# Score heads kept in different row strips, twelve exp tiles in flight, and head outputs turned by DMA: one change to a two-layer FFT-filter and attention kernel

## The chip, the core and the metric

The kernel runs on one core of a Trainium2 chip. A core has a matrix engine (TensorE, PE in the profile; its weight loads are listed as PEld), a vector engine (VectorE, DVE), a scalar engine (ScalarE, ACT), a general engine (GpSimd, POOL) and a sync engine (SP), which here only issues DMAs. Each engine runs its own list of instructions strictly in order and waits on semaphores for the others. The metric is the device time of one execution in microseconds (us).

## The reference

The input is a sequence of 2048 rows of 512 numbers in bf16. Two pairs of layers follow one another. The first layer of a pair filters in the frequency domain, the second is attention with 32 heads that share one key and one value head. Each works on the layer-normed rows and is added to them.

```python
S, D, H = 2048, 512, 32; Dh = 16
def _A_ref(x, w_r, w_i):
    X = rfft2(x) * (w_r + 1j * w_i)
    return irfft2(X, s=(S, D))
def _B_ref(x, wq, wk, wv, wo):
    q = (x @ wq).reshape(B, S, H, Dh).transpose(0, 2, 1, 3)
    k = x @ wk                      # one key head, 16 wide
    v = x @ wv
    scores = einsum("bhqd,bkd->bhqk", q, k) * Dh ** -0.5
    p = softmax(scores)
    o = einsum("bhqk,bkd->bhqd", p, v)
    return o.transpose(0, 2, 1, 3).reshape(B, S, H * Dh) @ wo
x = A_x
for _ in range(2):
    x = x + _A_ref(layernorm(x), A_w_r, A_w_i)
    x = x + _B_ref(layernorm(x), B_wq, B_wk, B_wv, B_wo)
```

## The kernel before, in words

The rows stay in SBUF in `x_sb`. The filter is done with matrix products against cosine and sine tables (`mm1`, `mid`, `inv`, `y_mm`) and radix-2 and radix-4 sums on VectorE (`radix2`, `radix4`). Nearly all the time goes into the attention.

**Units of attention work.** The queries are cut into four blocks `qb` of 512. The 32 heads are cut into four groups `g` of 8, and each group into two halves `par`, so a block is `(qb, g, par)`: 512 queries, 4 heads. There are 32 blocks a layer. The 2048 keys are cut into 16 chunks `kc` of 128. A unit is one head of one block against one key chunk: 64 units a block, 2048 a layer, 4096 in all.

**Scores.** `Emit.scores` (L1313 of the profile) multiplies a 32x128 slice of the keys (`KA` or `KB`) with a 32x512 slice of the queries. The head number `h` (0 to 3) picks the strip of 32 rows of the array that the product uses. Products in different strips run beside each other; two in the same strip run one after the other. In this text a slot is a set of such products in different strips, which the array does at one time.

**Exponentials, on two engines.** A pair of units goes to one of two two-bank PSUM tiles `sa` and through one exp on ScalarE (`Emit.exp`, L1318), which writes a 128x1024 bf16 tile `e2`. There are 13 such tiles, and the planner keeps at most `E_BUFS = 8` of them between scores and use. A single unit goes to a one-bank tile `b` and through VectorE: `p1` (L1325) makes a 16-bit integer whose bits are an approximate exponential. For every four units, two more integer tiles with an added constant are made (`phase`), nearly always on GpSimd (L1329); the three together average the error of the approximation out.

**Products with the values.** `Emit.pv` (L1335) multiplies a 128x32 slice of the values (16 columns of values, the rest ones, so that the softmax sum comes along) with the exponentials. Here the head picks a strip of 32 columns of the array. A ScalarE unit needs one such product, a VectorE unit three.

**Closing a block.** When all products of a block are there, VectorE turns the PSUM result in 32x32 squares (`evac`, L1342), and for each pair of blocks takes the reciprocal of the sums (`recip`, L1347), multiplies (`mul`, L1353) and turns the bf16 result back (`norm`, L1362) into `OT`, which is the stationary operand of the output projection `proj` (L1366). When the four groups of a `qb` are there, `close_rows` projects and adds the rows (`close_x`, L1248); in the first pair the front of the next filter layer (`mm1`, L1099, and `bn`, L1028) then follows among the attention work. A pair of row tiles is turned for that through DRAM: `turn_x` (L1070) writes `way`, `turned` (L1063) reads it with a transposing DMA.

**The order.** Nothing is scheduled by the compiler. `Plan` is a planner in Python with a price for every instruction. It keeps one clock for each engine and always emits the step that can start first. `do_scores` fills up to five score requests in a row, and for each takes the engine that would run dry first (`deadline`). `Attn.peek` says which heads of the current key chunk come next: for ScalarE the first two that are left, for VectorE one, preferably in a strip that is still free in the present slot. ScalarE gets no new scores while `live["ACT"]` has reached `bufs["ACT"]`. `round` gathers products with the values: it waits for four different heads unless the block is finished or a buffer limit is reached. `fill` puts products with zeros (L1010, L1014) on TensorE where it would do too little to keep its clock up. The result is one fixed list of instructions per engine.

Of the kernel before, what the change touches and what calls it, by code (L numbers as in the profile page):

```python
# [52 lines left out]
    return tabs  # L53


def radix2(nc, sd, x, piece):

    nc.vector.tensor_tensor(out=sd[:, 2 * piece:2 * piece + 2, :], in0=x[:, 0:2, :], in1=x[:, 2:4, :],
                            op=ALU.subtract if piece else ALU.add)


def radix4(nc, sd, x, half, o, piece):
# [53 lines left out]
class Plan:  # L116
# [12 lines left out]
    PORT = True  # L129
    POOL_LAG = 2600.0  # L130
    E_BUFS = 8
    T_BUFS = 4
    WIN = 3413.0
    WARM = 3500.0
# [11 lines left out]
    PATIENT = 1000.0  # L146
    URGE = 150.0
    TURN = 7000.0
    EARLY_SD = 0
    STARVED = 12000.0  # L150

    def __init__(self):
        self.t = {"PE": 0.0, "ACT": 0.0, "DVE": 0.0, "POOL": 0.0}
        self.mode = ""
        self.sa = [0.0, 0.0]
        self.bank = [0.0] * self.NB
        self.use = [None] * self.NB
        self.bg = {"PE": [], "ACT": [], "DVE": [], "POOL": []}
        self.n = 0
        self.hist = []  # L160
        self.at = None
        self.act_fifo, self.p1_fifo, self.ph_fifo, self.pool = [], [], [], []
        self.pv = []
        self.half = None
        self.live = {"ACT": 0, "DVE": 0}
        self.bufs = {"ACT": self.E_BUFS, "DVE": self.T_BUFS}
        self.dve_last = ""
        self.acc_of = {}
        self.bg_last = self.port = 0.0
        self.ranks, self.base = None, 0  # L170

    def ranked(self, which):
# [24 lines left out]
    def run(self, goal):  # L197
        while not goal():
            best = None
            for c in (self.pe_next(), self.act_next(), self.dve_next(), self.pool_next()):  # L200
                if c is not None and (best is None or c[0] < best[0]):
                    best = c
            best[1](best[0], *best[2:])


# [210 lines left out]
    def round(self):  # L416
        at = self.at
        avail = []
        free = self.slot_free("b")
        for e in sorted(self.pv, key=lambda e: e[:2]):  # L420
            if (e[2] in self.acc_of or free is not None) and e[4] // 4 in at.v_ready:
                avail.append((max(e[0], at.v_ready[e[4] // 4]),) + e[1:])
        if not avail:
            return None
        b0 = min(e[2] for e in avail)
        t0 = 0.0 if b0 in self.acc_of else free
        heads, sel = set(), []
        for e in avail:
            if e[2] == b0 and e[3] not in heads:
                heads.add(e[3])  # L430
                sel.append((max(e[0], t0),) + e[1:])
        if len(sel) < 4 and b0 + 1 in self.acc_of:
            for e in avail:
                if e[2] == b0 + 1 and e[3] not in heads:
                    heads.add(e[3])
                    sel.append(e)
        full = any(self.live[k] >= self.bufs[k] for k in ("ACT", "DVE"))
        return sel if len(sel) == 4 or self.made(b0) or full else None

    def made(self, b, h=None):  # L440
# [147 lines left out]
class Attn:  # L588
# [25 lines left out]
    def peek(self, kind, strips=()):  # L614


        cur = self.cur[kind]
        if not cur and self.groups:
            b, kc = self.groups[0]
            cur = [(b, kc, h) for h in range(4)]  # L620
        if not cur:
            other = self.cur["DVE" if kind == "ACT" else "ACT"]
            cur = other if kind == "DVE" or len(other) > 1 else []
        if kind == "ACT":
            return cur[:2]
        return sorted(cur, key=lambda u: u[2] in strips)[:1]

    def take(self, kind, us):
        if not self.cur[kind] and self.groups:
# [30 lines left out]
    def done(self, b, slot, end):  # L660
        p, em = self.plan, self.em
        qb, g, par = self.blocks[b]
        self.left.discard(b)
        m = Mark("PE", end, slot)
        ev = p.add("DVE", 630.0, [m], lambda k: em.evac(self, b, slot), give=(m,), prio=-3)
        self.evac[b] = self.evac_last = ev
        if par == 0:
            return
        tail = 0.0 if b >= len(self.blocks) - 2 else 5000.0
        rc = p.add("DVE", 260.0, [ev, self.evac[b - 1]], lambda k: em.recip(self, b), lazy=tail)  # L670
        mu = p.add("DVE", 600.0, [rc], lambda k: em.mul(self, b), lazy=tail, port=True)
        no = p.add("DVE", 626.0, [mu], lambda k: em.norm(self, b), lazy=tail)
        self.evac[b] = no
        if g == 3:
            self.layer.close_rows(qb, [self.evac[8 * qb + 2 * i + 1] for i in range(4)])


class Layer:
# [83 lines left out]

    def add_middle(self):
        p, em = self.plan, self.em
        self.mid, self.fil = [], []
        for u in range(4):
            evs, two = [], u in self.two

            if two:
                outs = [((0, 2), (0, 1), 0), ((1, 3), (0, 1), 2)]  # L770
            else:
                outs = [((0, 1, 2, 3), (0, 1), 0), ((0, 1, 2, 3), (2, 3), 2)]
            if u % 2:
# [27 lines left out]
    def add_back(self):  # L801
        p, em, at = self.plan, self.em, self.at
        left = [T]
        for t in range(T):
# [53 lines left out]
            def v_got(k, t=t):  # L858
                at.v_ready[t] = k.end + p.LAT[k.eng]
                left[0] -= 1  # L860
                if left[0] == self.EARLY:
                    at.dve_on = True
                    at.dve_from = k.end - 2000.0
# [61 lines left out]
class Emit:  # L925


    def __init__(self, ctx, tc, ins, out):
# [21 lines left out]
        self.part = const.tile([P, 2], F32, name="part")  # L950
        self.wv = const.tile([P, NC, DH], BF, name="wv")
        self.tc = tc
        self.e2 = [const.tile([P, 1024], BF, name=f"e2_{i}") for i in range(13)]
        self.idle, self.home, self.writer = list(range(13)), {}, {}
        self.WO = const.tile([P, 4, D], BF, name="WO")
        self.junk = const.tile([P, 512], BF, name="junk")
        self.eps = const.tile([P, 1], F32, name="eps")
# [197 lines left out]
    def turn(self, L, u, piece):  # L1155
        if piece == 0:
            L.sd_of[("x", u)] = self.t4([4, 512])
        radix2(self.nc, L.sd_of[("x", u)], L.X[u], piece)
        if piece:
            L.X[u] = L.sd_of.pop(("x", u))  # L1160

# [14 lines left out]

    def radix_d(self, L, u, piece):
        if piece == 0:
            L.Dz[u] = self.t4([4, 512], tag="xd", bufs=4)
        radix2(self.nc, L.Dz[u], L.X[u], piece)  # L1180

    def load_it(self, L, t):
        L.IT[t] = self.t4([4, 640], tag="it", bufs=2)
# [2 lines left out]
    def inv(self, L, t, b, j, slot, ks):  # L1186
# [4 lines left out]
        for k in ks:  # L1191
            u = 2 * j + k
            for a in range(2):
                for i in range(2):
                    w = 128 * (3 - (t * a + i) % 4)
                    z = L.Dz[u][:, 2 * (t % 2) + a, 256 * i + 128 * b:256 * i + 128 * b + 128]
                    self.nc.tensor.matmul(ps[:, k, :], lhsT=z, rhs=L.IT[t][:, u, w:w + 256], start=(a == 0 and i == 0),
                                          stop=(a == 1 and i == 1), skip_group_check=True)

    def inv0(self, L, b, j, slot, k):  # L1200

# [155 lines left out]
    def norm(self, at, b):  # L1357
# [3 lines left out]
            at.OT[qb] = self.t4([4, 512])  # L1361
        self.nc.vector.transpose(out=at.OT[qb][:, g, :], in_=on.rearrange("p a h d -> p (a h d)"))  # L1362

    def proj(self, at, t, r, slot, g0, g1):
        for g in range(g0, min(g1, 4)):
            self.nc.tensor.matmul(self.ps(slot), lhsT=at.OT[t][:, g, r * P:(r + 1) * P], rhs=self.WO[:, g, :],  # L1366
# [90 lines left out]
```

The softmax here doesn't subtract the row's maximum and nothing guards it: scores larger than these inputs give would overflow.

## Time and profile before

| what | value |
|---|---|
| runs shown | 1343.59, 1343.7 and 1344.19 us; median 1343.7 us |
| the profiled execution | span 1341.6 us, first to last instruction; it has no separate device time, so the span stands 2.1 us under the median of the runs |
| granted TensorE clock | 1.000 of full speed |
| attention of the first layer, last value slice (L1291) to last block closing (L1342) | 109.5 to 681.7 us |
| attention of the second layer, likewise | 774.9 to 1333.3 us |
| exp instructions on ScalarE (L1318) | 1232 |
| `p1` instructions on VectorE (L1325) | 1632 |
| transposes `norm` on VectorE (L1362) | 32 |

The page gives busy time by engine. Instructions of one engine overlap a little in its records: an exp lasts 1087 ns on average (group rows of L1318), but the next one can start 904 ns after it. So a wait shorter than about 180 ns does not show as idle time of ScalarE. Where this text speaks of a pitch, it is the time from the start of one instruction to the start of the next on that engine, read from the trace. Times of stretches are counted from the start of the span.

### The profile page before, as it was taken

How to read it: one execution, taken by the hardware profiler on the slowest of the kernel's cores; microseconds unless marked ns; L12 is line 12 of the kernel's file. 1: busy time of each engine (PE TensorE's matmuls, PEld its weight loads, DVE VectorE, ACT ScalarE, POOL GpSimd, SP SyncE). 2: the span in 40 equal slices, each digit the busy share in tenths (PEclk: the TensorE clock that was granted, in tenths of full speed). 3: DMA queues.
4: the chain of work that ended last, by engine and by line, in shares of the span. 5: the costliest groups of instructions: out<-in, count | busy, mean ns of one | idle time of the engine just before them, and what ended most of it. 6: DMA issues, size and time to landing. Idle time of an engine off the chain costs nothing. (4 is left out here: it accounts for less than half of the span.)

```text
span 1341.6 us, 31639 instructions
## 1 busy us (share of the span) xinstructions
PE 1310.9 (98%) x13046; PEld 428.0 (32%) x13046; DVE 1291.2 (96%) x2317; ACT 1225.7 (91%) x1390; POOL 849.7 (63%) x831
## 2 busy tenths in 40 slices
PE   9999999999999999999999999999999999999998
PEld 4642222222222222222246422222222222322222
DVE  6998999999999999999969999999999999999998
ACT  6478999999999999899954889999999999998996
POOL 0004777767776777667720068777777777876775
PEclk9999999999999999999999999999999999999999
DMA  9100000010001000100051000000000000000000
GB/s 292 41 1 1 2 1 2 2 33 1 2 2 33 1 2 2 32 2 2 1 165 41 1 1 1 2 2 6 13 2 2 6 13 2 2 1 17 1 1 17
DMA packets 29041, 25.16 MB, mean 19 GB/s; under 512 B 8672, under 2 KB 27616, under 8 KB 28896
## 3 DMA queue, kind: packets, MB, share of 16 engines
q1 hardware_dynamic: 28608, 22.58, 5.7%
q8 instruction: 102, 1.67, 0.5%
q10 hardware_dynamic: 288, 0.56, 0.1%
q14 instruction: 43, 0.35, 0.1%
HBM read 17.89 MB, written 3.67 MB: 16 GB/s over the span
## 5 line engine op out<-in xcount | busy, mean ns | idle before, releaser
L1313 PEld LDWEIGHTS <-KB 32*128 32x128 bf16 x2048 | 83.9, 91 | 224.0 <-issue 218.5
L1313 PEld LDWEIGHTS <-KA 32*128 32x128 bf16 x2048 | 82.3, 91 | 226.0 <-issue 217.8
L1335 PEld LDWEIGHTS <-vs_108 128*32 128x32 bf16 x2464 | 96.3, 94 | 111.3 <-issue 107.7
L1335 PEld LDWEIGHTS <-vs_109 128*32 128x32 bf16 x1632 | 96.3, 94 | 71.4 <-issue 69.0
L1335 PEld LDWEIGHTS <-vs_111 128*32 128x32 bf16 x1632 | 72.1, 94 | 72.7 <-issue 67.6
L1335 PEld LDWEIGHTS <-vs_110 128*32 128x32 bf16 x1632 | 70.0, 94 | 75.4 <-issue 71.9
L1329 POOL INT64_ADD w_1384<-w_1383 x1 | 1.0, 1041 | 110.5 <-DVE w_1383 L1325 110.5
L1329 POOL INT64_ADD w_10948<-w_10947 x1 | 1.0, 1039 | 97.7 <-DVE w_10947 L1325 97.7
L1318 ACT ACTIVATE e_2_86<-sa_65 128x1024 bf16<-128x1024 f32 x47 | 51.1, 1088 | 4.5 <-PE sa_64 L1313 4.0
L1318 ACT ACTIVATE e_12_96<-sa_65 128x1024 bf16<-128x1024 f32 x47 | 51.1, 1087 | 4.5 <-PE sa_64 L1313 4.1
L1318 ACT ACTIVATE e_5_89<-sa_65 128x1024 bf16<-128x1024 f32 x49 | 53.2, 1086 | 1.8 <-PE sa_64 L1313 1.0
L1318 ACT ACTIVATE e_7_91<-sa_64 128x1024 bf16<-128x1024 f32 x50 | 54.7, 1095 | 0.0
L1318 ACT ACTIVATE e_9_93<-sa_65 128x1024 bf16<-128x1024 f32 x49 | 53.2, 1086 | 1.6 <-PE sa_64 L1313 0.8
L1318 ACT ACTIVATE e_0_84<-sa_65 128x1024 bf16<-128x1024 f32 x47 | 51.7, 1101 | 3.2 <-PE sa_64 L1313 3.1
L1318 ACT ACTIVATE e_6_90<-sa_65 128x1024 bf16<-128x1024 f32 x49 | 53.1, 1083 | 1.5 <-PE sa_64 L1313 1.0
L1318 ACT ACTIVATE e_1_85<-sa_64 128x1024 bf16<-128x1024 f32 x50 | 54.2, 1083 | 0.0
L1318 ACT ACTIVATE e_3_87<-sa_65 128x1024 bf16<-128x1024 f32 x47 | 51.4, 1093 | 2.3 <-PE sa_64 L1313 2.0
L1318 ACT ACTIVATE e_11_95<-sa_65 128x1024 bf16<-128x1024 f32 x47 | 51.4, 1093 | 2.2 <-PE sa_64 L1313 1.9
L1318 ACT ACTIVATE e_4_88<-sa_65 128x1024 bf16<-128x1024 f32 x49 | 53.0, 1081 | 0.1
L1318 ACT ACTIVATE e_12_96<-sa_64 128x1024 bf16<-128x1024 f32 x48 | 52.7, 1099 | 0.2 <-PE sa_64 L1313 0.2
L1318 ACT ACTIVATE e_10_94<-sa_64 128x1024 bf16<-128x1024 f32 x49 | 52.5, 1072 | 0.1
L1318 ACT ACTIVATE e_3_87<-sa_64 128x1024 bf16<-128x1024 f32 x48 | 52.2, 1086 | 0.1
(4003 smaller groups left out, 6246.9 us busy)
## 6 DMA issues: line engine op xcount, KB each, us to landing
it<-const_IT SPq DMA_DIRECT2D x8, 640.0 KB, 6.3
x_sb<-in_A_x_dram SPq DMA_DIRECT2D x4, 512.0 KB, 6.9
out_dram<-x_sb SPq DMA_DIRECT2D x16, 128.0 KB, 1.8
way<-x_sb SPq DMA_DIRECT2D x6, 256.0 KB, 2.2
tab_PH<-const_PH ACTq DMA_DIRECT2D x1, 512.0 KB, 5.1
w_123<-const_FT SPq DMA_DIRECT2D x1, 512.0 KB, 8.8
w_128<-const_FT SPq DMA_DIRECT2D x1, 512.0 KB, 8.5
tab_PS<-const_PS SPq DMA_DIRECT2D x1, 512.0 KB, 7.9
```

Of the source, the lines that this page charges most:

```text
L1313: self.nc.tensor.matmul(o, lhsT=KX[rs, kc * P:(kc + 1) * P], rhs=at.QT[qb][rs, g, :], start=True, stop=True, skip_group_check=True)
L1318: self.wrote("ACT", e, self.nc.scalar.activation(out=e, in_=self.ps(slot), func=ACT.Exp, scale=SCALE))
L1329: self.nc.gpsimd.int64_add(t[p][:, 0:n].bitcast(U64), t[0][:, 0:n].bitcast(U64), DELTA[p] * FOUR)
L1335: self.nc.tensor.matmul(self.ps(slot)[32 * h:32 * h + 32, :], lhsT=V[:, kc, :], rhs=rhs, start=first, stop=last, skip_group_check=True)
```

## The change

Three things are done to the planner and the emitter, with what they need around them.

First, `peek` takes the strips into account for both engines: ScalarE's two heads are chosen among those whose strips are free in the present slot, and, after that, so that they differ from the last heads that the other engine still holds.

Second, the limit on ScalarE tiles in flight becomes 12 from the moment that all value slices of a layer are there, and goes back to 8 where the next filter layer's middle part is planned. The pool grows from 13 to 21 tiles of `e2`. The sums of `radix_d`, which had four tiles `xd` of their own, now use two `e2` tiles each and give each back after its last use.

Third, for all pairs of blocks but the last of a layer the transpose `norm` is replaced by `norm_dma`: four DMAs write the result to DRAM in runs of 64 bytes, and a transposing DMA reads it back into `OT`. The planner reckons with 25 us from `mul` until the projection may use it. All five are issued on SP.

If no engine has anything that it may do, the planner now lets `round` go with fewer than four heads once.

```diff
 class Plan:
     E_BUFS = 8
+    E_LATE = 12
+    OUT_TURN = 25000.0
...
 def run(self, goal):
+            if best is None:
+                assert not self.force
+                self.force = True
+                continue
+            self.force = False
             best[1](best[0], *best[2:])
...
 def round(self):
-        full = any(self.live[k] >= self.bufs[k] for k in ("ACT", "DVE"))
+        full = self.force or any(self.live[k] >= self.bufs[k] for k in ("ACT", "DVE"))
...
 def peek(self, kind, strips=()):
+        taken = lambda x: {u[2] for u in self.cur[x]} if 0 < len(self.cur[x]) <= 2 else ()
         if kind == "ACT":
-            return cur[:2]
-        return sorted(cur, key=lambda u: u[2] in strips)[:1]
+            d = taken("DVE")
+            return sorted(cur, key=lambda u: (u[2] in strips, u[2] in d))[:2]
+        a = taken("ACT")
+        return sorted(cur, key=lambda u: (u[2] in strips, u[2] in a))[:1]
...
 def done(self, b, slot, end):
-        no = p.add("DVE", 626.0, [mu], lambda k: em.norm(self, b), lazy=tail)
+        if b < len(self.blocks) - 2:
+            no = Mark("DMA", None)
+
+            def turned(k):
+                em.norm_dma(self, b)
+                no.end = k.end + p.OUT_TURN
+
+            mu.then = turned
+        else:
+            no = p.add("DVE", 626.0, [mu], lambda k: em.norm(self, b), lazy=tail)
...
 def add_middle(self):
+        p.bufs["ACT"] = p.E_BUFS
...
 def v_got(k, t=t):
+                if left[0] == 0:
+                    p.bufs["ACT"] = p.E_LATE
...
-        self.e2 = [const.tile([P, 1024], BF, name=f"e2_{i}") for i in range(13)]
+        self.e2 = [const.tile([P, 1024], BF, name=f"e2_{i}") for i in range(21)]
...
 def radix_d(self, L, u, piece):
         if piece == 0:
-            L.Dz[u] = self.t4([4, 512], tag="xd", bufs=4)
-        radix2(self.nc, L.Dz[u], L.X[u], piece)
+            L.Dz[u] = [[self.t2([2, 512]), 4] for _ in range(2)]
+            for z, _ in L.Dz[u]:
+                self.writer.pop(self.home[id(z)][0], None)
+        radix2(self.nc, L.Dz[u][piece][0], L.X[u], piece)
...
 def inv(self, L, t, b, j, slot, ks):
+            d = L.Dz[u][t % 2]
+            d[1] -= 1
+            if d[1] == 0:
+                self.free2(d[0])
...
+    def norm_dma(self, at, b):
+        qb, g, par = at.blocks[b]
+        on = at.raw.pop((qb, g))
+        if g == 0:
+            at.OT[qb] = self.t4([4, 512])
+        way = self.way.tile([512, P], BF, name="onw", tag="onw")
+        rows = way.rearrange("(a q) (h c) -> h q a c", q=32, c=32)
+        for h in range(4):
+            self.nc.sync.dma_start(out=rows[h], in_=on[32 * h:32 * h + 32].rearrange("p a h d -> p a (h d)"))
+        self.nc.sync.dma_start_transpose(out=at.OT[qb][:, g:g + 1, :], in_=way)
```

More of the change, by code (lines that the diff above doesn't have):

```diff
@@ L53, in host_tables, with radix2 @@
     return tabs
-def radix2(nc, sd, x, piece):
-    nc.vector.tensor_tensor(out=sd[:, 2 * piece:2 * piece + 2, :], in0=x[:, 0:2, :], in1=x[:, 2:4, :],
-                            op=ALU.subtract if piece else ALU.add)
+def radix2(nc, o, x, piece):
+    nc.vector.tensor_tensor(out=o, in0=x[:, 0:2, :], in1=x[:, 2:4, :], op=ALU.subtract if piece else ALU.add)
 def radix4(nc, sd, x, half, o, piece):
@@ L202, in run @@
                     best = c
+            if best is None:
+                assert not self.force
+                self.force = True
+                continue
+            self.force = False
             best[1](best[0], *best[2:])
@@ L952, in __init__ @@
         self.tc = tc
-        self.e2 = [const.tile([P, 1024], BF, name=f"e2_{i}") for i in range(13)]
-        self.idle, self.home, self.writer = list(range(13)), {}, {}
+        self.e2 = [const.tile([P, 1024], BF, name=f"e2_{i}") for i in range(21)]
+        self.idle, self.home, self.writer = list(range(21)), {}, {}
         self.WO = const.tile([P, 4, D], BF, name="WO")
@@ L1157, in turn @@
             L.sd_of[("x", u)] = self.t4([4, 512])
-        radix2(self.nc, L.sd_of[("x", u)], L.X[u], piece)
+        radix2(self.nc, L.sd_of[("x", u)][:, 2 * piece:2 * piece + 2, :], L.X[u], piece)
         if piece:
@@ L1195, in inv @@
                     w = 128 * (3 - (t * a + i) % 4)
-                    z = L.Dz[u][:, 2 * (t % 2) + a, 256 * i + 128 * b:256 * i + 128 * b + 128]
+                    z = L.Dz[u][t % 2][0][:, a, 256 * i + 128 * b:256 * i + 128 * b + 128]
                     self.nc.tensor.matmul(ps[:, k, :], lhsT=z, rhs=L.IT[t][:, u, w:w + 256], start=(a == 0 and i == 0),
                                           stop=(a == 1 and i == 1), skip_group_check=True)
+            d = L.Dz[u][t % 2]
+            d[1] -= 1
+            if d[1] == 0:
+                self.free2(d[0])
     def inv0(self, L, b, j, slot, k):
```

## The prediction

> **What bounds the kernel now.** I read the page's first part, then stretches of the trace, then the waits of ScalarE.
>
> ```profile
> PE 1310.9 (98%) x13046; PEld 428.0 (32%) x13046; DVE 1291.2 (96%) x2317; ACT 1225.7 (91%) x1390; POOL 849.7 (63%) x831
> ```
>
> Three engines look nearly full. The two long stretches below are quiet attention; the seven short ones are where rows of a query block are closed.
>
> ```profile
> core 0: us, PE busy (x) PEld busy (x) DVE busy (x) ACT busy (x) POOL busy (x), PEclk, DMA share, GB/s
> 200.00:250.00 50.00, 49.42 (x527) 14.57 (x523) 50.00 (x86) 49.94 (x56) 39.06 (x39) 1.00 0.01 1
> 1000.00:1050.00 50.00, 49.80 (x544) 14.06 (x536) 49.88 (x84) 50.00 (x56) 39.51 (x39) 1.00 0.01 1
> 278.00:284.00 6.00, 6.00 (x62) 1.81 (x60) 5.93 (x13) 3.86 (x5) 3.07 (x3) 1.00 0.14 46
> 429.00:451.00 22.00, 22.00 (x215) 6.12 (x213) 21.40 (x40) 19.88 (x23) 12.59 (x15) 1.00 0.01 1
> 553.00:561.00 8.00, 7.55 (x54) 2.45 (x55) 7.97 (x16) 3.98 (x5) 3.65 (x4) 1.00 0.12 37
> 943.00:948.00 5.00, 4.78 (x43) 1.52 (x39) 5.00 (x10) 3.41 (x4) 3.13 (x4) 1.00 0.08 28
> 1078.00:1083.00 5.00, 5.00 (x45) 1.43 (x47) 4.14 (x8) 3.95 (x5) 3.78 (x4) 1.00 0.08 26
> 1209.00:1225.00 16.00, 15.77 (x123) 4.18 (x121) 14.10 (x24) 12.00 (x14) 9.53 (x10) 1.00 0.10 33
> 1247.00:1252.00 5.00, 4.81 (x33) 1.37 (x35) 4.91 (x9) 3.01 (x5) 4.20 (x5) 1.00 0.01 3
> ```
>
> In quiet attention VectorE and ScalarE are both full (50.00 and 49.94 of 50 us), so both bound it: what leaves one is shared out by moving units to it from the other. In the seven closings (67 us) ScalarE is busy 50.1 us and idle 16.9; VectorE is idle 3.5. One of these waits:
>
> ```profile
> 279.69 1.02 ACT L1318 ACTIVATE e_9_93<-sa_64 128x1024 bf16<-128x1024 f32 x1
> 282.79 1.02 ACT L1318 ACTIVATE e_12_96<-sa_65 128x1024 bf16<-128x1024 f32 x1 [2.08 <-PE sa_64 L1313]
> ```
>
> ScalarE waits 2.08 us for scores that TensorE, in order, has not issued. Walking TensorE's instruction list, I counted units scored into `sa` but not yet multiplied with the values: it stands at 16, the limit of 8 tiles, in this wait, and reaches 14 to 16 in the other six closings except the last (13). The limit stops ScalarE there, while TensorE does projections and `mm1`.
>
> **TensorE: a row and a rule.** The row says 98%. Read so, TensorE is the bound. But the Trainium skill ("Trainium Kernel Development and Optimization", Performance Expectations) calls matmul busy time a bad metric because matmuls are pipelined, and wants weight-load busy time instead: here 32%. I settled it from starts in the trace. A run of products in one slot takes 321 ns, in two slots 532 to 548: 216 ns a slot and some 105 for changing the kind of product. Slots are counted from the strips in the instruction list: 1628 for scores, 1850 for values, 1014 for the rest (512 columns each), in 2458 runs: 4492 x 0.216 + 2458 x 0.105 = 1228 us, 92% of the span. TensorE has about 8% to spare, spread thinly. By the row alone its saving would count in full (first rival); by the account it doesn't.
>
> **The change part by part.** Both instruction lists can be compared; counts below are from them.
>
> *Strips.* Score slots fall from 1628 to 1449, runs of all kinds from 2458 to 2428: 179 x 0.216 + 30 x 0.105 = 41.8 us off TensorE. It covers nothing directly, since VectorE and ScalarE are the bound; its worth is that scores and late products come sooner. Score runs of four products in two slots fall from 305 to 167. Zero products go from 66 full and 40 quarter ones to 64 and 48: 76 slots both times, so I leave the clock at its 1.00.
>
> *Norm.* 30 of 32 transposes leave VectorE.
>
> ```profile
> L1362 DVE STREAM_TRANSPOSE w_1951<-on x4: 697/698/698, 148.8 to 256.9; 128x512 bf16<-128x512 bf16 x4
> ```
>
> They last 698 ns, but the next instruction starts 625 ns after: 30 x 0.625 = 18.8 us. None is at a place where VectorE idles: no engine idle time stands before them. The two that end a layer stay.
>
> *Units.* `p1` goes from 1632 to 1622, exps from 1232 to 1238. Pitches: `p1` 0.598, exp 0.904. VectorE loses another 6.0 us; ScalarE gains 5.4. One whole `phase` (2.09 us) on VectorE becomes four single-unit ones; at a quarter each, about 0.17 us by its size, that is 1.4 us less. So VectorE's own work falls by 18.8 + 6.0 + 1.4 = 26.2 us, ScalarE's rises by 5.4.
>
> *Twelve tiles.* Over the two attention stretches (572.2 and 558.5 us) I summed the least pitch of each kind of instruction: VectorE 557.5 and 546.6, ScalarE 544.5 and 532.5. So VectorE loses 14.7 and 11.9 us to waiting, ScalarE 27.7 and 26.0. Of ScalarE's 53.7 the closings are 16.9, plus some 2.7 of pitch that idle time doesn't show (15 waits by 0.18); about 14 are the start of P1 work and the layers' ends, which the change leaves; about 20 are waits below 250 ns. In the new list the count of units in flight peaks at 24, the new limit, once, and at 20 to 22 in most closings, so the limit no longer stops ScalarE: 19.6 us can go. Of the 20 us of small waits I give 8 to the eased TensorE (bounds 0 and 20; no row shows it, and the strips are the only thing that touches them).
>
> *The DMA way.* Per pair of blocks five DMAs on SP, 150 in all. Nearest rows:
>
> ```profile
> way<-x_sb SPq DMA_DIRECT2D x6, 256.0 KB, 2.2
> e_8_92<-way SPq DMA_TRANSPOSE x2, 3.5
> ```
>
> Four issues of 0.4 us, 2.2 us to land, then the transpose 3.5: 7.3 us. It carries 128 KB and the row 256, but in runs of 64 bytes. The skill speaks against that ("DMA: Bandwidth & Descriptors", Specifications: under 512 bytes a write becomes read-modify-write). The trace's packets take 9 ns at 32 bytes, 18 at 256, 27 at 512: no penalty shows below 512, though those are not short writes to DRAM. By the rows 2048 runs over 16 engines add 128 x 0.01 = 1.3 us, about 9 in all; doubling for the rule 10; at the 59 ns of a 1280-byte packet 15. The cover: between the last `mul` of a query block and the first `add_x` that needs it, the new VectorE list holds 26.4 to 29.6 us of work, and 21 us after the last DMA-turned pair of a layer. So it costs nothing by row or rule. Without cover TensorE would wait in order at `proj`, with all scores queued behind it. On SP, row writes of `x_sb` and the input loads of the next layer queue behind these five; their places in SP's list follow the plan, and a `way` pair is late by 5 us at most, before a front that has as much spare. The transpose that opens an `OT` tile waits for the tile's former users; only SP stands behind it. `mul` now waits for DMA reads of `on` two pairs back, over 20 us old.
>
> *radix_d in e2.* Same 16 sums. The lists of VectorE around the filter's middle are identical, so 0; the bound is the 3.9 us that weight loads wait for `xd` (gain) and as much again (loss).
>
> **The sum.** The list is fixed, so both engines must fit. VectorE: -26.2 plus new waits. ScalarE: +5.4 less what it stops losing: 19.6 + 8 = 27.6, so -22.2. The slower one sets it: -22, VectorE then waiting 4 us more than now. Against the profiled 1341.6 that is 1319.6; the median of the runs stands 2.1 above the span, so 1321.7.
>
> **Rivals.** (1) *TensorE is the bound after all*: -41.8 us, 1302. For: 98%, and waits named after L1313. Against: full VectorE and ScalarE in the quiet stretches; -26 is all that VectorE's list gives, unless its own 26.6 us of waits shrink as well, to perhaps -33. Chance 0.10 for anything beyond -29 (1300 to 1315).
>
> (2) *The waits move instead of going*: ScalarE runs ahead by four tiles, but the backlog must be multiplied later and stops it then. If half of 19.6 and none of the small ones go: +5.4 - 9.8 = -4.4, 1339; with all of the 19.6 and no small ones -14. Chance 0.22 for -3 to -14 (1329 to 1341); for: TensorE has no idle stretch to catch up in; against: 41.8 us less work for it.
>
> (3) *Slower: ScalarE is the bound with more to do.* Six more exps stand in its list. If the closings' waits come from TensorE's order of projections and not from the limit, they stay, and the time grows by 5.4: 1349. It decides where less than 5.4 of ScalarE's 53.7 us go. Against it: the count of 16 in flight in the waits. Chance 0.05.
>
> (4) *The DMA way isn't covered*: from 26.4 us on, three closings a layer each stop TensorE by the excess; at 40 us 6 x 13.6 = 82 lost. The highest bound above is 15. Chance 0.02.
>
> **How the numbers follow.** My case, -14 to -29, has 0.58 (1315 to 1329). About 0.2% (2.7 us) is what a measurement of this kernel can tell from no change. Slower by more: 0.05 + 0.02, less a little that stays inside: 0.06. Same: 0.03. Faster: 0.91. The range reaches from rival 1's near part (1310) into rival 2 (1336).
>
> **What would show it.** Right: in a closing ScalarE idles under 0.5 us; VectorE still above 49.5 of 50 us in quiet stretches; ScalarE's 53.7 us down to about 26; 2 transposes of L1362's kind; proj not waiting for DMA; transposing DMAs landing within 6 us. Wrong: closings with ScalarE idle as before (rival 2 or 3); a TensorE wait for `onw` (4); VectorE with gaps in quiet stretches; a span under 1310, which would say that TensorE held both.

## The result, and the profile after

The changed kernel takes 1332.68 us (median of 4 runs, 1332.57 to 1332.93) against 1343.87 us for the kernel before on the same chip: 11.2 us less, ratio 0.9917 with a 95% interval of 0.9903 to 0.9931. The forecast was 1321.7, range 1310 to 1336. So the sign and the range held, and the gain was half of the forecast one. The case that the prediction held most likely, 14 to 29 us less, did not come. Where the other 11 us are is the subject of the rest.

The page of the changed kernel: the span, and busy time by engine.

```profile
span 1330.8 us, 31765 instructions
...
PE 1291.0 (97%) x12968; PEld 438.2 (33%) x13032; DVE 1273.3 (96%) x2280; ACT 1226.4 (92%) x1396; POOL 842.0 (63%) x826
```

VectorE is busy 17.9 us less than before, ScalarE 0.7 us more, in a span 10.8 us shorter. The stretches of the trace follow (after the times: the length, then the busy us of TensorE, its weight loads, VectorE, ScalarE and GpSimd with their instructions). The two of 50 us are quiet attention; 278, 429, 943, 1085 and 1225 are closings; 926 and 1068 are one and the same place in two query blocks.

```profile
core 0: us, PE busy (x) PEld busy (x) DVE busy (x) ACT busy (x) POOL busy (x), PEclk, DMA share, GB/s
200.00:250.00 50.00, 48.57 (x525) 14.83 (x522) 49.68 (x85) 49.94 (x56) 39.38 (x39) 1.00 0.07 9
...
278.00:284.00 6.00, 5.52 (x47) 1.66 (x46) 5.93 (x13) 6.00 (x8) 2.16 (x3) 1.00 0.45 100
429.00:451.00 22.00, 21.17 (x213) 6.09 (x208) 21.75 (x40) 21.97 (x27) 12.55 (x14) 1.00 0.27 61
...
926.00:931.00 5.00, 4.64 (x50) 1.63 (x47) 2.88 (x6) 3.43 (x5) 3.22 (x4) 1.00 0.01 3
943.00:948.00 5.00, 5.00 (x65) 1.32 (x61) 5.00 (x10) 5.00 (x6) 4.34 (x6) 1.00 0.19 23
1068.00:1073.00 5.00, 4.64 (x50) 1.69 (x47) 2.88 (x5) 3.43 (x4) 2.90 (x3) 1.00 0.00 0
1085.00:1090.00 5.00, 5.00 (x63) 1.36 (x61) 5.00 (x9) 5.00 (x7) 4.34 (x5) 1.00 0.24 39
...
1225.00:1235.00 10.00, 10.00 (x129) 2.73 (x126) 9.98 (x17) 10.00 (x12) 8.20 (x8) 1.00 0.19 29
...
1000.00:1050.00 50.00, 48.57 (x521) 14.74 (x520) 49.67 (x85) 49.94 (x55) 39.32 (x38) 1.00 0.07 10
```

In quiet attention VectorE is busy 49.67 of 50 us, still full. In the closings ScalarE is busy 47.97 of 48 us; before, it stood idle for a quarter of such stretches. So the waits that the forecast named are gone. But there is a new kind: at 926, 1068 and (not shown) 268 and 1210 us VectorE stands idle for 2.1 of 5 us, ScalarE for 1.6, away from any closing. Here is the one at 926 us in the timeline (start, duration, engine, line, operation, output from input; in brackets the idle time before it and what ended it):

```profile
927.71 1.35 ACT L1346 ACTIVATE e_20_104<-sa_64 128x1024 bf16<-128x1024 f32 x1
...
928.36 1.41 PEld L1325 LDWEIGHTS <-wq 128*128 128x128 bf16 x8 [0.42 <-issue]
928.59 0.81 PE L1325 MATMUL b_69<-gx,wq 128*128 128x512 bf16 x3 [0.16 <-issue]
...
929.24 1.03 PE L1325 MATMUL b_68<-gx,wq 128*128 128x512 bf16 x4
929.44 0.69 DVE L1285 CAST w_12390<-b_69 128x512 bf16<-128x512 f32 x1 [1.95 <-PE b_69 L1325]
930.19 0.11 PEld L1341 LDWEIGHTS <-KA 32*128 32x128 bf16 x6 [0.42 <-DVE w_12390 L1285]
930.20 0.39 PE L1341 MATMUL sa_65<-w_12390,KA 32*128 32x512 bf16 x2
...
930.63 1.02 ACT L1346 ACTIVATE e_8_92<-sa_65 128x1024 bf16<-128x1024 f32 x1 [1.57 <-PE sa_64 L1341]
```

L1325 is the query projection, four products for one group of 8 heads. Two of them (8 weight loads) are done in one go at the moment when the scores have run out. VectorE must copy the first (L1285) before the next scores (L1341) can be made, and only then does ScalarE get work. In the second attention of the kernel before, every query projection stands alone; in the changed one three of eleven lots have eight products.

How much is that? I repeat the account of the prediction: for each engine the least pitch of each kind of instruction, summed over the two attention stretches (564.9 and 553.9 us after; 572.2 and 558.5 before). The rest is waiting. Rare kinds make it uncertain by some 3 us.

| both attention stretches, us | before | after | change | forecast |
|---|---|---|---|---|
| VectorE, own work | 1104.1 | 1080.4 | -23.7 | -26.2 |
| ScalarE, own work | 1077.0 | 1081.2 | +4.2 | +5.4 |
| ScalarE, waiting | 53.7 | 37.6 | -16.1 | -27.6 |
| VectorE, waiting | 26.6 | 38.4 | +11.8 | +4 |

The own work came out as forecast within the account. The waits did not: together they fell by 4.3 us and not by 23.6. Of the 19.3 us between, the four places above are 4 x (2.03 + 2.01) = 16.2 (start of one instruction to the next, less its least pitch). Without these four places ScalarE's waits would have fallen by 24.1 us and VectorE's risen by 3.7, near the forecast. Half of 19.3, since both engines share the work, is 9.7 us of time.

The DMA way, by DMA issues (how many, size, median us from issue to landing):

```profile
onw<-on SPq DMA_DIRECT2D x120, 32.0 KB, 1.9
way<-x_sb SPq DMA_DIRECT2D x6, 256.0 KB, 2.4
w_1890<-onw SPq DMA_TRANSPOSE x4, 2.4
```

And the writes on SP (shortest, median and longest issue in ns):

```profile
L1401 SPq DMA_DIRECT2D onw<-on x120: 315/489/1557, 145.2 to 1300.7; - x120
```

The four writes land in 1.9 us each, their issue takes 0.49 us of SP's time apiece, the transposing read lands in 2.4 to 2.8 (medians by `OT` tile; the longest of all took 4.0): some 6.3 us in all, against a cover of 26. The 61440 packets of 64 bytes that the writes consist of took 8 ns each (median), no more than the 9 ns of 32 bytes. No wait of a computing engine names `onw`; only SP waits, for the writes, before it issues the read.

### The profile page after: what moved, and what is told of

Read it like the earlier page. It is cut to its first block, busy times and chain, and to the rows that moved or that the text cites. A ratio compares the mean times of both kernels' runs of the same rounds, so it can differ in the third digit from the quotient of the medians.

```text
span 1330.8 us, 31765 instructions
## 1 busy us (share of the span) xinstructions
PE 1291.0 (97%) x12968; PEld 438.2 (33%) x13032; DVE 1273.3 (96%) x2280; ACT 1226.4 (92%) x1396; POOL 842.0 (63%) x826
## 5 line engine op out<-in xcount | busy, mean ns | idle before, releaser
L1341 PEld LDWEIGHTS <-KA 32*128 32x128 bf16 x2048 | 87.6, 91 | 234.1 <-issue 222.9
L1341 PEld LDWEIGHTS <-KB 32*128 32x128 bf16 x2048 | 85.2, 91 | 229.7 <-issue 224.1
L1363 PEld LDWEIGHTS <-vs_116 128*32 128x32 bf16 x2474 | 98.3, 94 | 97.2 <-issue 90.8
L1363 PEld LDWEIGHTS <-vs_117 128*32 128x32 bf16 x1622 | 97.7, 94 | 62.8 <-issue 60.6
L1363 PEld LDWEIGHTS <-vs_118 128*32 128x32 bf16 x1622 | 71.0, 93 | 75.6 <-issue 72.8
L1363 PEld LDWEIGHTS <-vs_119 128*32 128x32 bf16 x1622 | 72.0, 94 | 65.5 <-issue 57.5
L1050 DVE BATCH_NORM_STATS2 st<-x_sb 128x6 f32<-128x512 bf16 x52 | 35.4, 681 | 4.1 <-DMA x_sb<-in_A_x_dram 3.6
L1346 ACT ACTIVATE e_8_92<-sa_65 128x1024 bf16<-128x1024 f32 x32 | 35.5, 1110 | 2.4 <-PE sa_64 L1341 1.6
L1346 ACT ACTIVATE e_6_90<-sa_64 128x1024 bf16<-128x1024 f32 x33 | 36.5, 1106 | 0.0
L1346 ACT ACTIVATE e_13_97<-sa_65 128x1024 bf16<-128x1024 f32 x31 | 34.7, 1118 | 1.6 <-PE sa_64 L1341 1.6
L1346 ACT ACTIVATE e_1_85<-sa_64 128x1024 bf16<-128x1024 f32 x32 | 35.4, 1107 | 0.0
L1346 ACT ACTIVATE e_5_89<-sa_65 128x1024 bf16<-128x1024 f32 x30 | 33.5, 1118 | 1.6 <-PE sa_64 L1341 1.6
L1346 ACT ACTIVATE e_12_96<-sa_65 128x1024 bf16<-128x1024 f32 x31 | 34.1, 1100 | 0.9 <-PE b_69 L1341 0.8
L1346 ACT ACTIVATE e_19_103<-sa_65 128x1024 bf16<-128x1024 f32 x31 | 34.7, 1121 | 0.1
L1346 ACT ACTIVATE e_10_94<-sa_65 128x1024 bf16<-128x1024 f32 x30 | 33.2, 1106 | 1.7 <-PE sa_64 L1341 1.6
L1346 ACT ACTIVATE e_18_102<-sa_64 128x1024 bf16<-128x1024 f32 x31 | 34.6, 1115 | 0.1
L1346 ACT ACTIVATE e_2_86<-sa_65 128x1024 bf16<-128x1024 f32 x30 | 33.5, 1116 | 1.3 <-PE sa_64 L1341 1.0
L1346 ACT ACTIVATE e_9_93<-sa_64 128x1024 bf16<-128x1024 f32 x31 | 34.6, 1115 | 0.1
L1346 ACT ACTIVATE e_7_91<-sa_65 128x1024 bf16<-128x1024 f32 x31 | 34.4, 1110 | 0.1
L1346 ACT ACTIVATE e_15_99<-sa_64 128x1024 bf16<-128x1024 f32 x31 | 34.3, 1107 | 0.1
```

What stands on the lines that cost most here:

```text
L1050: self.nc.vector.bn_stats(st, self.ps(slot) if slot else self.x[:, x[1], x[0], :])
L1341: self.nc.tensor.matmul(o, lhsT=KX[rs, kc * P:(kc + 1) * P], rhs=at.QT[qb][rs, g, :], start=True, stop=True, skip_group_check=True)
L1346: self.wrote("ACT", e, self.nc.scalar.activation(out=e, in_=self.ps(slot), func=ACT.Exp, scale=SCALE))
L1363: self.nc.tensor.matmul(self.ps(slot)[32 * h:32 * h + 32, :], lhsT=V[:, kc, :], rhs=rhs, start=first, stop=last, skip_group_check=True)
```

## Experiments

**Theory A:** the shortfall is the late query projections, and moving them gives it back. **Rival B:** TensorE is short of time everywhere, so a wait that is taken away comes back at the next late step. **Rival C:** parts of the change are worth little or nothing, the DMA way above all.

### The parts, one left out

The edits: `E_LATE = 8` (eight_tiles); the old `peek` (old_strips); `no = p.add("DVE", 626.0, [mu], lambda k: em.norm(self, b), lazy=tail)` for all blocks (no_dma_way). Each is planned anew.

> Changed kernel with the limit of 8 tiles kept for the whole attention; strips and the DMA way are kept. Theory (the limit stopped ScalarE in closings, and raising it gave the 16.1 us less waiting of ScalarE): waits of ScalarE rise by about 16 us, half of which lands in the time: about 1340, with closings in which ScalarE stands idle for 2 us again at 16 units in flight. Rival (the waits would have gone with the strips alone, since TensorE has 42 us less to do): within 2 us of 1332.7.

> Changed kernel with the old choice of heads; twelve tiles and the DMA way are kept. Score slots rise from 1449 to about 1635, 40 us more of TensorE's time. Theory of the prediction (TensorE has 8% to spare, so only small waits return): 1338 to 1342. Rival 1 (TensorE is the bound): about 1372. Between: a TensorE without slack puts each late step off, 1345 to 1360.

> Changed kernel, but the transposes stay on VectorE (30 x 0.625 = 18.8 us back); strips and twelve tiles are kept. Planned anew, it has 1610 p1 and 1243 exps (changed kernel: 1622 and 1238). Theory (VectorE and ScalarE bind, work is shared between them): half of 18.8 less what is now planned elsewhere, so about 9 us over the changed kernel: 1342. Rival (TensorE is what the engines wait for, so VectorE's relief is worth little): at most 3 us over it, up to 1336.

### The parts, one alone

The kernel before with one part of the change: the new `peek` (strips_alone), `norm_dma` (dma_alone), `E_LATE = 12` (tiles_alone). `radix_d` in `e2` is in all of them.

> Kernel before with the new choice of heads alone (8 tiles, transposes on VectorE). Score slots fall from 1628 to 1467, 35 us of TensorE's time; 1626 p1 and 1235 exps, so the work of VectorE and ScalarE is about as before. Theory (TensorE only sets how long the other two wait, and at 8 tiles the limit stops ScalarE anyway): 0 to 3 us under before, 1341 to 1344. Rival (TensorE is the bound): 35 us under, 1309.

> Kernel before with the DMA way alone (old choice of heads, 8 tiles): 30 transposes leave VectorE, 18.8 us. Planned with 1652 p1 and 1222 exps: p1 +20 x 0.598 = 12.0 us, exps -10 x 0.904 = -9.0. The prediction's reading (VectorE and ScalarE both bind, so what leaves VectorE is shared out): -7 to -9, about 1336. Rival, after the first four runs (VectorE's relief asks for scores sooner than TensorE with the old choice of heads can bring them): no gain or a loss, 1343 to 1349.

> Kernel before with the limit of 12 tiles alone (old choice of heads, transposes on VectorE): 1614 p1, 1241 exps. The prediction's reading (the limit's stops of ScalarE, 19.6 us, go): VectorE loses 18 p1, 10.8 us, so up to -10: 1334. Rival (the backlog must be multiplied later by a TensorE without slack, and the waits move): -2 to +3, 1342 to 1347.

Together they make all eight combinations. Waits are by the account above. In three kernels the clock falls in some executions and the times scatter: at a mean granted clock of 0.999 or more dma_alone takes 1345.92 to 1346.46 us, old_strips 1344.45 to 1345.89 and eight_tiles 1339.07 to 1340.59; at a lower one they go up to 1351.61, 1356.62 and 1346.98. The waits of dma_alone are from an execution at 0.995 (1351.61 us), those of old_strips from one at 0.998 (1345.84), so some of them are that. The last column is where the planner's own clocks (`Plan.t`) stand when its list is done; its prices are constants and know nothing of the granted clock.

| strips | DMA way | 12 tiles | us | ratio to before, 95% | VectorE waits | ScalarE waits | planner, us |
|---|---|---|---|---|---|---|---|
| | | | 1343.87 | | 26.6 | 53.7 | 1347.2 |
| x | | | 1346.59 | 1.0021 [1.0013, 1.0029] | 29.9 | 55.1 | 1345.3 |
| | x | | 1347.90 | 1.0027 [1.0017, 1.0038] | 34.8 | 70.8 | 1351.0 |
| | | x | 1335.79 | 0.9939 [0.9924, 0.9954] | 24.7 | 38.9 | 1339.0 |
| x | x | | 1340.39 | 0.9981 [0.9972, 0.9989] | 32.8 | 49.6 | 1338.7 |
| x | | x | 1340.81 | 0.9976 [0.9967, 0.9986] | 33.4 | 42.2 | 1339.0 |
| | x | x | 1346.28 | 1.0035 [1.0023, 1.0047] | 44.4 | 50.1 | 1348.8 |
| x | x | x | 1332.68 | 0.9917 [0.9903, 0.9931] | 38.4 | 37.6 | 1330.6 |

Against what was expected: eight_tiles, no_dma_way and tiles_alone came near their theories (1340, 1342 and 1334), though ScalarE's waits rose by 12.0 us in eight_tiles and not by 16. old_strips fell between its theory and its rival, where a TensorE without slack puts each late step off. strips_alone missed both (0 to 3 us less were expected, 2.7 more came), and dma_alone came as its rival had it.

*Twelve tiles* are the part that pays by itself: -8.1 us, with 14.8 us of ScalarE's waits gone. The expectation was "up to -10"; the rival of moved waits falls. Taken away from the changed kernel they cost 7.7 us, and ScalarE is stopped in closings again, at 16 units in flight, as expected of the limit. (The count is that of score products into `sa` less value products from `e`, in TensorE's order in the trace. In the kernel before it reaches 16 in all seven closings, also in the last, for which the prediction has 13.) The stretches of eight_tiles:

```profile
1097.00:1105.00 8.00, 8.00 (x73) 2.40 (x70) 7.41 (x13) 4.82 (x6) 4.56 (x6) 1.00 0.23 66
1236.00:1243.00 7.00, 6.70 (x49) 2.32 (x48) 6.16 (x11) 3.58 (x5) 3.96 (x4) 1.00 0.44 96
```

ScalarE is idle 6.6 of 15 us in these two closings. In tiles_alone, with up to 24 units in flight, no closing has a wait of ScalarE over 0.5 us.

*The DMA way* is a loss of 4.0 us alone (2.1 to 2.6 at a clock of 0.999 or more) and of 10.5 on top of the twelve tiles, but a gain of 6.2 on top of the strips and of 8.1 on top of both. *The strips* lose 2.7 alone and gain 13.6 on top of the other two. The waits point to the reason. With the old heads the DMA way raises VectorE's waits by 8.2 and 19.7 us and ScalarE's by 17.1 and 11.2; with the new heads VectorE's rise by 2.9 and 5.0 only and ScalarE's fall. A VectorE with less to do asks for scores sooner; at 1626 to 1635 score slots TensorE cannot bring them, at 1447 to 1449 it nearly can. This reading is from the waits; no run changed the score slots alone in a fixed list. The planner's clocks have the same interplay (+3.8 and +9.8 us for the DMA way with the old heads, -6.6 and -8.4 with the new), so it lies in the order of the lists and needs no lower clock. One stretch of old_strips shows both engines idle at full clock with TensorE busy:

```profile
956.00:966.00 10.00, 9.82 (x80) 3.07 (x80) 6.68 (x12) 8.07 (x9) 3.48 (x5) 1.00 0.20 55
```

ScalarE's two waits in it come at 22 and at 24 units in flight, where the new limit of 12 tiles is. The late projections come with the new heads: lots of eight products stand once in strips_alone, three times in no_dma_way and in eight_tiles and four times in the changed kernel; with the old heads once in dma_alone and in old_strips and nowhere in the kernel before and tiles_alone.

### How far an order moves the time by itself

One constant: `OUT_TURN = 26000.0` instead of `25000.0`.

> The changed kernel with one constant changed: the planner reckons with 26 instead of 25 us for the DMA way. The work is the same (1619 p1, 1239 exps), the way itself too; only the order differs, from the first closing on. It measures how far an order planned anew moves the time by itself. Theory (the missing or extra waits at closings depend on how the order happens to fall, so part of what single parts bring or cost is that): 2 to 5 us away from the changed kernel. Rival (the order is robust, and the differences of the parts are the parts' own): within 1 us of it, 1332 to 1334.

It took 1335.22 us, 2.5 over the changed kernel at the same work. In the trace the attentions are as long as the changed kernel's (564.6 and 553.9 us), and the stretch between them (last closing of the first to last value slice of the second) is 95.6 us instead of 93.2. So a difference of 2 to 3 us between two kernels that were planned anew (strips_alone against before, and dma_alone at full clock) need not be the part's own; the differences of 6 to 14 us above are larger than that, but were tried with one order each.

### VectorE's transposes back, in the same list

```diff
 def norm_dma(self, at, b):
+        self.nc.vector.transpose(out=self.scr, in_=on.rearrange("p a h d -> p (a h d)"))
         for h in range(4):
             self.nc.sync.dma_start(out=rows[h], in_=...)
```

> The changed kernel's list unaltered, with the 30 VectorE transposes put back where they stood, into a scratch tile that nobody reads; the DMA way stays and is still what is used. VectorE has 30 x 0.625 = 18.8 us more. Theory (VectorE's list binds and has 38 us of waits in attention, few of them just behind a closing): 60 to 100% of it, +11 to +19: 1344 to 1352. Rival (the relief of VectorE was worth little, since the waits for TensorE take it up): +0 to +6, 1333 to 1339.

```profile
L1401 DVE STREAM_TRANSPOSE scr<-on x30: 711/711/714, 145.2 to 1313.5; 128x512 bf16<-128x512 bf16 x30
```

It took 1348.60 us, 15.9 more than the changed kernel: 85% of 18.8. VectorE got more than that, though, 22 us by the account: a transpose right behind `mul` moves the next start after `mul` from 0.598 to 0.713 us and takes 0.636 itself. Of 22 us it is 72%. VectorE's waits fell by 6.3 us and ScalarE's rose by 14.5. Rival C falls for the changed kernel: in a fixed list, most of the time on VectorE counts.

### Less wait for the query projection, in the same list

```diff
 def qt_mm(self, at, key, slot, c):
+        if g in (1, 2) and c < NC - 1:
+            return
-                              start=(c == 0), ...
+                              start=(c == 0 or g in (1, 2)), ...
```

> The changed kernel's list unaltered, but the query projections of groups 1 and 2 do one of their four contraction steps (so the other three quarters of those queries' sums are left out). TensorE has 16 x 3 x 0.216 = 10 us less to do; at the four query-block boundaries where both engines wait 2.0 us, six of the eight projection products go. Theory (these late projections cost their own time on both engines): each wait shrinks by 1.3 to 1.4 us, the time by 5 to 6 us: 1327. Rival (TensorE is short all around, the wait only moves to the next late step): 0 to 2 us less, 1331 to 1333.

1334.72 us, 2.0 more than the changed kernel: neither the theory nor the rival. ScalarE's and VectorE's waits at the four places did shrink, from 2.01 and 2.03 to 1.36 and 1.38. That is three products (3 x 0.216), not six: the second projection is done while VectorE copies the first, as the timeline above shows. And the missing products cost elsewhere, at the start of the first attention:

```profile
108.00:112.00 4.00, 2.62 (x31) 1.12 (x30) 2.27 (x7) 1.71 (x3) 0.00 (x0) 1.00 0.00 0
112.00:116.00 4.00, 3.39 (x17) 0.70 (x15) 3.91 (x7) 3.88 (x4) 2.06 (x2) 0.79 0.00 0
116.00:120.00 4.00, 4.00 (x29) 0.70 (x28) 1.91 (x4) 2.46 (x3) 2.06 (x2) 0.50 0.00 0
```

The granted clock (third number from the end) falls to 0.50, and VectorE and ScalarE starve. In the changed kernel it is 1.00 there. It falls twice more, for 3.4 us each (551.2 and 776.5 us). Four of the five executions had a mean clock of 0.995; the fifth, with the same list at 0.998, took 1331.07 us, 1.6 less than the changed kernel. So the next kernel leaves the layer's start alone and also takes away the wait for VectorE's copy:

```diff
 def qt_mm(self, at, key, slot, c):
+        cut = qb > 0 and g in (1, 2)
+        if cut and c < NC - 1:
+            return
...
 def scores(self, at, slot, us):
-            ... rhs=at.QT[qb][rs, g, :], ...
+            ... rhs=at.QT[qb][rs, 0 if qb and g == 1 else g, :], ...
```

> The changed kernel's list unaltered, but in the later three query blocks of a layer the projections of groups 1 and 2 do one of four contraction steps, and the scores of group 1 read the queries of group 0 (so group 1's own scores are left out); the start of a layer is as it was. TensorE has 7.8 us less to do. At the four boundaries where both engines wait 2.0 us, 2 of 8 projection products and no wait for VectorE's copy remain, about 0.5 us. Theory (the late query projections are what is missing of the forecast): -4 to -7 against the changed kernel, 1326 to 1329, with the four waits at 0.5 us. Rival (the wait moves on to the next late step): -2 to 0, 1331 to 1333.

1330.11 us: 2.6 less than the changed kernel, between the two expectations. ScalarE's wait at the four places is 0.72 us now, VectorE's still 1.38: its copy stands in its list and waits for the projection, which in TensorE's list still comes last. The timeline of query_free:

```profile
929.13 1.29 DVE L1285 CAST w<-b 128x512 bf16<-128x512 f32 x2 [1.30 <-PE b L1366]
...
929.67 2.87 ACT L1349 ACTIVATE e<-sa 128x1024 bf16<-128x1024 f32 x3 [0.27 <-PE sa L1344]
```

The second attention fell by 2.7 us (551.2), the first by 0.1, where a clock of 0.50 from 548.7 to 552.1 us took back what was won. In the second attention each of three places gave VectorE 0.65 us and ScalarE 1.29; three times the mean of the two is 2.9. So a late projection costs the mean of what the two engines wait, as in the account above, and to be rid of it the projection must come sooner, not be shorter.

### The query projection sooner

In `pe_next`, ahead of the rule that urgent scores go first (it returns scores before it looks at projections, each time an engine is about to run dry):

```diff
+            due = [b for b in self.bg_next("PE") if b[3].order == 1 and b[3].parts == 4 and T - b[3].born > 8000 and ...]
+            if due and self.scored and limit > T - 200:
+                self.scored = False
+                return (due[0][0],) + due[0][2:6] + (1,)
             if limit < T - self.LATE and first <= T + self.PE_SW:
                 return (first, self.do_scores)
...
 def do_scores(...):
+        self.scored = True
```

> The changed kernel, planned anew with one more rule: a query projection asked for over 8 us ago gets one contraction step after each fill of scores, as long as no engine is about to run dry. 1617 p1, 1240 exps, the same 1844 to 1861 value slots. Theory (the late query projections are what the forecast missed, 4 x 2.0 us of both engines): the four waits go and no others come, -4 to -8 against the changed kernel: 1325 to 1329. Rival (TensorE is short there, so that the waits come back at the next closing): -2 to +2, 1331 to 1335.

1332.32 us, 0.4 from the changed kernel, which taken alone would be the rival's number. The stretches say otherwise. The second attention fell from 553.9 to 548.3 us, with no wait at query blocks; the first rose from 564.9 to 571.3 in the profiled execution, mostly for this:

```profile
296.00:300.00 4.00, 1.84 (x11) 0.35 (x10) 2.45 (x5) 1.71 (x2) 2.05 (x2) 0.80 0.54 131
300.00:304.00 4.00, 4.00 (x24) 0.65 (x21) 1.53 (x3) 3.02 (x5) 0.00 (x0) 0.50 0.36 66
```

In the first closing of the new order TensorE has a gap (busy 1.84 of 4 us), and its clock is 0.50 from 298.4 us on for 10.2 us, in which both other engines starve. The gap is a wait for a DMA (L1127 is `mm1`, L1098 the write of the rows to `way`, L1408 the transposing read of `onw`):

```profile
291.14 1.84 SPq L1408 DMA_TRANSPOSE w<-onw  x1
293.03 0.57 SPq L1098 DMA_DIRECT2D way<-x_sb  x1
...
298.81 1.03 PE L1127 MATMUL b<-tab_PH,e 128*128 128x512 bf16 x2 [2.16 <-DMA e<-way]
```

VectorE had these rows done at 291.49 us, but SP was issuing the read of the heads' results until 292.98, so they left 1.5 us late. The DMA way is not free where an order leaves the rows no spare. The planner's clocks, which know neither SP's queue nor the granted clock, have 1326.4 us for this list; its executions took 1330.76 us (mean clock 0.999) to 1338.87 (0.991). So the rule was kept for the second pair of layers alone (`due and T > 700000.0 and self.scored`), which has the same 592 exps and 817 `p1` in its attention either way.

> The changed kernel, planned anew with the rule of query_early in the second pair of layers alone, so that the first pair keeps the changed kernel's order. 1622 p1 and 1238 exps, the same numbers as the changed kernel. Theory (in the second attention the three waits of both engines at query blocks are the late projections; query_early had that stretch at 548.3 us instead of 553.9 at the same work, and lost 6.4 in the first attention by the order there and a lower clock): first attention 565, second 548 to 549, so -5 to -6: 1327. Rival (query_early's gain in the second attention was luck of the order): second attention 552 to 556, so -2 to +2, 1331 to 1335.

1327.46 us (1327.17 to 1327.65): 5.2 less than the changed kernel, ratio to before 0.9876 [0.9859, 0.9892], the fastest of all. First attention 564.8, second 548.6; the waits of both attentions are 32.9 us (VectorE) and 31.0 (ScalarE). The two places in the second attention that were shown idle above:

```profile
926.00:931.00 5.00, 5.00 (x64) 1.49 (x66) 4.87 (x9) 5.00 (x6) 4.17 (x5) 1.00 0.01 3
...
1068.00:1073.00 5.00, 4.99 (x68) 1.40 (x65) 4.87 (x9) 5.00 (x7) 4.10 (x5) 1.00 0.00 0
```

VectorE is busy 4.87 of 5 us instead of 2.88, ScalarE 5.00 instead of 3.43. Three waits of 2.03 us are 6.1; 5.3 of it came through to the stretch. Theory A holds where it was tried by moving the projections alone, in the second attention. The fourth place, in the first attention, was left as it is, and what it would give was not shown.

## Why the prediction was right or wrong

*Right: VectorE's and ScalarE's own work.* -26.2 and +5.4 were forecast, -23.7 and +4.2 came. That work off VectorE counts was shown by norm_added, where 72% of the added work came through.

*Right: the limit of 8 tiles is what ScalarE waits for in closings.* Those waits went, twelve tiles alone bring 8.1 us, and with 8 tiles the waits are back at 16 units in flight.

*Right for the changed kernel: the DMA way is covered.* 6.3 us against 7.3 to 10; no computing engine waits. That `way` has as much spare as it may be late holds for this order and not for that of query_early. The Trainium skill's rule ("DMA: Bandwidth & Descriptors", Specifications) that a write under 512 bytes becomes a read-modify-write shows no price here: runs of 64 bytes to DRAM land in 1.9 us for 32 KB, 256 KB of `way` in 2.4, and a packet of 64 bytes took 8 ns. *radix_d at nothing*: between the attentions the time is 93.2 us before and after.

*Wrong: the term for waits.* "19.6 + 8 = 27.6" off ScalarE was 16.1, and "VectorE then waiting 4 us more" was 11.8. The step that failed is that I asked only which waits the change takes away, and gave the new order none of its own. I had counted VectorE's and TensorE's instructions in the new list, but did not ask where each query projection stood in it: four places with eight L1325 products in a row, just ahead of a new group's first scores, were there to be read. So were the planner's own clocks: in the new list they hold ScalarE idle for 1.99 us and VectorE for 2.09 at each of the four places, and they end 16.6 us sooner than in the old one (1330.6 against 1347.2), not 22. The 19.3 us of waits too many, shared by two engines, are 9.7 of the 11.2 us by which the span, 1330.8, missed the forecast's 1319.6. The own work is 0.7 of it (1.3 too much, shared by two), and the end after the last closing, 9.2 us instead of 8.2, another 1.0, whose cause is open. The three add up to 11.4; the account is no finer than that.

*Wrong: "It covers nothing directly", of TensorE's 41.8 us.* Alone it does bring nothing (+2.7). But it is what lets the DMA way pay: without it the DMA way costs time at either limit. An account in which TensorE is 92% full, averaged, did not show that the other engines' lists can be shortened only while it keeps up.

*The rivals.* (1) TensorE as the bound would have given 1302, and did not come; old_strips, with 186 more score slots, 40 us of TensorE's time, lost 13.6, so a third of it counts in that direction. That the range of the forecast held is in part luck, since it reached into the numbers of rival (2). (2) gave the right number, -3 to -14, by a cause that was only half right: waits did appear elsewhere, but for a projection that the order put off, not for a backlog of products with the values. They did not have to, which also ends rival B for these waits: query_early_second has them neither in the closings nor at the three query blocks. (3) and (4) fell, since the closings' waits went and no computing engine waits for `onw`.

## What to carry to other kernels

When a change takes waits away from a fixed order, look in the new list for the steps that used to hide in those waits (projections, copies, anything with low rank), and ask of each how long before its first use it now stands. Split time into own work and waiting for each of the engines that share the work: the halved sum is the time, and an instruction moved, a wait gone and a wait come can be set off against each other. Where a planner in the program lays out the list, read its clocks before a sum is done by hand: here they had the four new waits, and the right sign for six of the seven combinations. Judge the parts of a planned kernel in combination and against the scatter of another order, since here two of three parts lost time alone and the three together won 11 us.

## What the runs showed of the hardware that was not expected

TensorE's clock fell to half without a long gap. The Trainium skill ("TensorE: Matmul & The Clock Gate", Why this matters for your kernels) advises to have no idle gaps above some 3 us. In query_free TensorE's longest gap between 545 and 549 us was 0.5 us (starts and ends in the timeline), and it was busy 2.85 of 4 us, mostly with 32-row products; then the clock was 0.50 until 552.1:

```profile
545.00:549.00 4.00, 2.85 (x25) 0.94 (x22) 4.00 (x8) 4.00 (x5) 3.66 (x4) 0.97 0.15 33
549.00:553.00 4.00, 4.00 (x36) 0.71 (x33) 2.79 (x6) 3.09 (x4) 2.08 (x3) 0.61 0.00 0
```

In dma_alone the longest gap before such a fall was 0.2 us:

```profile
189.10:193.10 4.00, 3.71 (x20) 0.87 (x18) 3.88 (x8) 3.34 (x4) 3.10 (x4) 1.00 0.00 0
193.10:199.90 6.80, 6.80 (x46) 1.09 (x45) 4.88 (x8) 3.76 (x4) 3.41 (x4) 0.50 0.01 2
```

VectorE and ScalarE, which TensorE feeds, lost time at these places. The rule's gap is not the limit in this case, and what is stays open. The share of the array at work, estimated from each product's columns and strips, does not tell the cases apart: it is 0.24 to 0.44 in the 4 us before the eight falls of all runs, and 0.27 to 0.40 at its lowest in the kernels without one (from 30 us on).
